# Memory and x queries through one p\*v pass and one output projection per step, with A's weight strips kept in DRAM in SBUF layout

## The chip, the cores and the metric

The kernel runs on one core of a Trainium2 chip. The metric is the device time of one execution in microseconds (us). The core has a matrix engine (TensorE, PE in the profile; its weight loads are PEld), VectorE (DVE), ScalarE (ACT), GpSimd (POOL), and SyncE (SP), which here only issues DMAs. PE multiplies a stationary operand (lhsT), which it has loaded as weights, with a moving one, and writes to PSUM, of which the kernel uses eight banks of 128 x 512 float32. ACT and DVE move results from there to SBUF.

## The reference

Four layers follow each other on x of 2048 rows and 576 columns, each with a layernorm before it and a residual around it: A, B, A, B, with the same weights in both A and both B.

```python
x = x + _A_ref(_layernorm(x), A_wqkv, A_wo)
x = x + _B_ref(_layernorm(x), B_mem0, B_Wq, B_Wk, B_Wv, B_Wo, B_seg_len)
x = x + _A_ref(_layernorm(x), A_wqkv, A_wo)
x = x + _B_ref(_layernorm(x), B_mem0, B_Wq, B_Wk, B_Wv, B_Wo, B_seg_len)
```

A is attention with 32 heads of 18 columns over a dilated window: position s sees s, s-2, ..., s-14. B has 32 heads of 128 columns and goes over 64 segments of 32 rows one after the other. It carries a memory of 8 rows from segment to segment:

```python
mem = mem0
for s in range(n_seg):
    h = concatenate([mem, x[:, s*32:(s+1)*32]])      # 8 + 32 rows
    q, k, v = h @ Wq, h @ Wk, h @ Wv                   # 32 heads x 128
    p = softmax(where(mask, q @ k.T * scale, -1e9))    # memory queries see all; x queries see memory and are causal
    o = (p @ v) @ Wo
    mem = o[:8]                                        # the next segment's memory
    outs.append(o[8:])
```

So a segment of B can't begin its products before the eight output rows of the segment before it are there.

## The kernel before

**Lanes and steps.** Both B layers run at once, as two lanes. Lane 0 is the first B layer and is at segment t in step t; lane 1 is the second and is at segment t - DLY (6 before). There are 64 + 6 = 70 steps, 6 at each end with one lane alone. A tile of 64 rows of layer A (32 tiles for each of the two A layers) is worked in between: the first A layer a few steps ahead of lane 0, the second between lane 0 and lane 1.

**A step of B.** `hT` holds the step's input, transposed, in 80 columns: 32 of lane 0's x, 8 + 8 memory rows of both lanes, 32 of lane 1's x. `qk` (L757, L759) makes q and k: for each head and each of the two, 5 matmuls with 128 x 128 weights and 80 moving columns (40 with one lane), 320 a step in 11 groups of three heads. `vpass` (L803) makes v for blocks of 32 rows, 40 matmuls of 512 columns a block. `scores` runs four times a step: for halves r = 0 and 1 of 16 heads each, and for kinds "m" (memory queries) and "x" (the rows of x). It first puts the mask into the bank by matmuls (L836), then adds q k (L848), column-tiled: four matmuls of 32 output rows side by side. `softmax` goes over three engines: maximum and subtraction on DVE, exponential on ACT, sum and reciprocal on DVE, the scaling on DVE for m and on POOL for x, and a transpose in 32 x 32 blocks on DVE (L712) into `ptm` or `ptx`.

**p\*v and projection.** `pv_m` (L872) runs once per half for the memory queries of both lanes: 48 matmuls of 16 moving columns, row-tiled (32 rows of V each, four side by side, into four banks). `pv_x` (L912) runs once a step for the x queries of both halves: 96 matmuls of 32 or 64 columns. Their results go to the tile `OT`. `oproj` (L946) multiplies OT with wo, 160 matmuls in eight parts. Its columns in step t are the memory queries of step t and the x queries of step t - 1: `pv_x` of a step comes after that step's projection. `mem_out` copies the memory rows into the next step's `hT`, `x_out` adds the x rows to the residual. After the last step one projection for the last x queries follows.

**A's weights.** A's projections don't stay in SBUF. `wload` (L442, L444) brings them in twelve strips per tile (nine of wqkv, three of wo) into a ring of three buffers, with two DMAs a strip: one of rows of up to 508 or 512 bytes for the first 512 rows of the weight, one for the last 64.

**The order.** Nothing is ordered by the engines' own choice: each piece of work is declared as an operation with an engine, an estimated time, dependencies, buffers and a priority (a due time in steps, from the table `PR`). A planner (`_Plan.run`) goes through a modelled time, gives each free engine the ready operation with the lowest priority number whose buffers are free, and writes the instructions in that order. It knows an extra time (`SWITCH`) when PE changes between full-width, column-tiled and row-tiled work.

Of the kernel before, what the change touches and what calls it, by code (L numbers as in the profile page):

```python
# [9 lines left out]
BF16 = mybir.dt.bfloat16  # L10
# [37 lines left out]
class _Op:  # L48
    __slots__ = ("eng", "us", "lat", "fn", "prio", "seq", "acq", "uses", "wait", "next", "mode", "tmin", "done", "lk")


class _Plan:
# [20 lines left out]
    def op(self, eng, us, fn, prio, deps=(), acq=(), uses=(), lat=None, mode="F", tmin=0.0, lk=False):  # L73
# [3 lines left out]
        o.fn, o.prio, o.lat, o.mode, o.tmin, o.lk = fn, prio, lat, mode, tmin, lk  # L77
# [12 lines left out]
    def run(self, log=None):  # L90
# [23 lines left out]
        port = 0.0  # L114
        while left:
# [92 lines left out]
class _K:  # L208
# [37 lines left out]
    def setup(self):  # L246
# [7 lines left out]
        self.x3T = dp.tile([P, NT, 5, T], F32, name="x3T")  # L254

        self.ident = ident = cp.tile([P, P], BF16, name="ident")
        nc.gpsimd.memset(ident[:], 1.0)
        self.sel(ident[:], [[-1, P]], 1, 0, ALU.is_equal, 0.0)
        self.ones = ones = cp.tile([P, P], BF16, name="ones")
# [61 lines left out]
        self.pl.pool("OTm", [None])  # L321
        self.pl.pool("OTx", [None])
        tiles("qk", 7, [P, 3, 2, W80])
        tiles("ptm", 2, [P, 4, 3, 32])
        tiles("ptx", 2, [P, 2, 4, 2, 32])
# [25 lines left out]
        tiles("ot", 1, [P, D])  # L351
        for t_ in tiles("ring", 3, [P, 5, 256]):
            nc.vector.memset(t_[64:128, 4, :], 0.0)
# [3 lines left out]
    def prologue(self):  # L357
# [36 lines left out]
        b = pl.op("PE", 0.3, tr, -2.0, [a], acq=[ps], uses=[x0], mode="R")  # L394
# [8 lines left out]
    def layernorm(self, xT, dep, prio, writer, wus, wacq=(), wuses=(), early=False):  # L403
# [14 lines left out]
        c = pl.op("PE", 0.28, mm, prio, [a, b], acq=[ps], uses=[xs])  # L418
# [16 lines left out]
    def wload(self, src, rows, col0, n, prio, dep):  # L435

        w = self.pl.buf("ring")
        step, last = rows

        def ld(e):  # L440
            d, f = self.nc.sync.dma_start, src[0:1, col0:col0 + 1]
            d(out=w.t[:, 0:4, 0:n], in_=bass.AP(f.tensor, f.offset, [[src.shape[1], P], [step * src.shape[1], 4], [1, n]]))  # L442
            k = min(P, src.shape[0] - last)
            d(out=w.t[0:k, 4, 0:n], in_=src[last:last + k, col0:col0 + n])  # L444
        o = self.pl.op("SP", 0.9, ld, prio, [dep], acq=[w], lat=4.0)
        return w, o

    def a_tile(self, layer, j, dep, due, span):
# [8 lines left out]
        if layer == 1:  # L457
# [9 lines left out]
            b = pl.op("PE", 0.16, tr, pr(0.04), [a], acq=[ps, xT], uses=[x0])  # L467
# [21 lines left out]
        for part in (0, 1, 2):  # L489
            ps = pl.buf("r")  # L490
            o = o_n
            for c in range(5):
                if c % 2 == 0:
                    w, ow = self.wload(self.A_wqkv, (P, 512), part * D + CB[c], 254 if c < 4 else P, pr(Q[1]) - PR["ring"], gate)
                w0 = c % 2 * CB[1]

                def mm(e, c=c, w=w, ps=ps, w0=w0):
                    for kc in range(5):
                        nc.tensor.matmul(ps.t[:, c * T:(c + 1) * T], lhsT=w.t[:, kc, w0:w0 + P], rhs=xn.t[:, kc, :],  # L499
                                         start=(kc == 0), stop=(kc == 4))  # L500
                o = pl.op("PE", 0.15, mm, pr(Q[1] + 0.03 * part), [o, ow], acq=[ps, dst[part]] if c == 0 else (),
                          uses=[xn, w] if c == 0 else [xn, w, ps], lat=0.0 if c < 4 else None)
# [47 lines left out]
        o = o_l = pl.op("PE", 0.4, logits, pr(Q[3]), [o], acq=[psL, e_], uses=[big], mode="C")  # L550
# [26 lines left out]
        for n, (c0, nb) in enumerate(((0, 2), (2, 3))):  # L577
            ps = [pl.buf("r") for _ in range(NQ)]
            b = pl.op("PE", 0.09 * nb, lambda e, ps=ps, c0=c0, nb=nb: spread(ps, c0, nb), pr(Q[4] + 0.02 * n), [b], acq=ps,
                      uses=[e_], mode="R")  # L580
# [20 lines left out]
        for mb in range(5):  # L601
            if mb % 2 == 0:
                w, ow = self.wload(self.A_wo, (CB[1], CB[4]), mb * P, 256 if mb < 4 else 64, pr(Q[6]) - PR["ring"], o_l)
            w0 = mb % 2 * P

            def mm(e, mb=mb, w=w, ps=ps, w0=w0):
                for c in range(5):
                    nc.tensor.matmul(ps.t[:, mb * T:(mb + 1) * T], lhsT=w.t[:, c, w0:w0 + P], rhs=oT.t[:, c, :], start=(c == 0), stop=(c == 4))  # L608
            o = pl.op("PE", 0.15, mm, pr(Q[6]), [o, ow], acq=[ps] if mb == 0 else (),
                      uses=[oT, w] if mb == 0 else [oT, w, ps], lat=0.0 if mb < 4 else None)  # L610
# [8 lines left out]
        def wr2(e, m, rstd):  # L619
# [5 lines left out]
            for o, i, bc in views:  # L625
# [4 lines left out]
                  pr(Q[7]), [o], uses=[xnb])  # L630
        lane = 0 if layer == 1 else 1
# [12 lines left out]
    def finish_out(self, j, prio):  # L644
        nc, pl = self.nc, self.pl
        xb, ot = self.acc[1][j][2], pl.buf("ot")
        a = self.x_done[1][NS * j + NS - 1]
        for n, (c0, c1) in enumerate(((0, 4), (4, 5))):
# [6 lines left out]
            b = pl.op("PE", 0.06 * (c1 - c0), tr, prio, [a], acq=[ps] + ([ot] if n == 0 else []), uses=[xb])  # L655
# [8 lines left out]
        pl.op("SP", 0.5, lambda e: nc.sync.dma_start(out=self.out[0, j * T:(j + 1) * T, :], in_=ot.t[0:T, :]), prio, [o],  # L664
# [13 lines left out]
    def softmax(self, t, ps, e_, n, prio, dep, mul, view, eview, tview, last, pt):  # L678
# [28 lines left out]
        def mult(e):  # L707
# [4 lines left out]
        return pl.op("DVE", 0.14 + 0.00112 * last, lambda e: nc.vector.transpose(out=pt.t[:].rearrange(  # L712
            "p i b q -> p i (b q)" if len(pt.t.shape) == 4 else "p l i b q -> p (l i) (b q)"), in_=tview(e_.t)),
            prio, [o], acq=[pt], uses=[e_])
# [27 lines left out]
    def qk(self, t, g, prio):  # L742
# [8 lines left out]
        def mm(e):  # L751
            pv = ps.t[:, 0:480].rearrange("p (h w k) -> p h w k", h=3, w=2)
            for hh, h in enumerate(heads):
                for wi in range(2):
# [7 lines left out]
                  {h // 8 for h in heads}] if t == 0 else []), acq=[ps, sb], uses=[hT])  # L762
# [209 lines left out]
    def x_out(self, t, dep, prio):  # L972

        nc, pl, psY = self.nc, self.pl, self.psY
        if t < 0:
            return
# [145 lines left out]
```

## Time and profile before

| | |
|---|---|
| median of 3 runs | 2414.54 us (2412.74 to 2416.62) |
| the profiled execution: its own time | 2408.13 us |
| its span, first to last instruction | 2406.4 us |
| mean granted clock of PE | 0.986 |
| matmuls on PE | 70669 |
| PE busy | 2170.3 us (90% of the span) |
| DVE, ACT, POOL busy | 62%, 47%, 42% |
| moved by DMA | 242.42 MB in 508286 packets |

In rows of the profile, "L757" is line 757 of the kernel before, "r<-hT,wq" says that a PSUM bank r is written from tiles hT and wq, "x48" is a count. A row in order of time gives the start, the length up to the last one's end, and in brackets the idle time before it and what ended it. PE's matmuls overlap, so that a group's rate is read from starts. "issue" means that the engine waited for nothing that the profile shows.

### The profile page before, as it was taken

What the parts mean: (1) busy time and instruction counts of PE and PEld (TensorE: products, weight loads), DVE (VectorE), ACT (ScalarE), POOL (GpSimd) and SP (SyncE); (2) the same over time, 40 slices, a digit from 0 to 9 for tenths busy, and PEclk for the clock granted to TensorE, in tenths of its full rate; (3) what the DMA queues carried; (4) which work ended last, traced back from release to release, by engine and by line L of the source; (5) the groups of instructions that cost most, each with busy time, mean ns of one, the idle gap of its engine ahead of it and who ended that gap; (6) DMA issues with size and microseconds to landing.
All of it is one profiled execution on the core that took longest, in us unless ns stands there. A gap on an engine that the chain in (4) does not pass through costs nothing.

```text
span 2406.4 us, 154586 instructions
## 1 busy us (share of the span) xinstructions
PE 2170.3 (90%) x70669; PEld 1862.4 (77%) x70669; DVE 1484.4 (62%) x3777; ACT 1132.6 (47%) x2952; POOL 1006.6 (42%) x1316
## 2 busy tenths in 40 slices
PE   2689999999999999999999999999999999999998
PEld 1577778887788788778787888888888888788876
DVE  3366656666666666666666656666676566665664
ACT  1244444444544444444455444554454445444443
POOL 3142443544454444444454444444444444443320
PEclk9999999999999999999999999999999999999999
DMA  8643443344344434433444344433443443442220
GB/s 244 186 106 84 99 99 96 96 106 108 87 101 103 108 84 110 106 90 94 103 115 101 90 103 107 101 96 101 111 99 92 106 102 93 99 102 62 63 65 11
DMA packets 508286, 242.42 MB, mean 101 GB/s; under 512 B 400744, under 2 KB 503152, under 8 KB 507632
## 3 DMA queue, kind: packets, MB, share of 16 engines
q1 hardware_dynamic: 502800, 213.67, 36.3%
q0 software_dynamic: 4832, 18.88, 2.4%
q8 instruction: 552, 9.04, 1.6%
q14 instruction: 102, 0.84, 0.1%
HBM read 219.59 MB, written 12.85 MB: 97 GB/s over the span
## 4 chain that ended last, share of the span: by engine, by line
PE 85%; issue 6%; DMA 6%; DVE 2%; ACT 1%; SPq 0%; POOL 0%; ACTq 0%; DVEq 0%; POOLq 0%
PE r L757 27%; PE r L946 15%; PE r L803 15%; PE r L759 6%; PE r L499 6%; DMA ring<-in_A_wqkv_dram 6%; PE r L912 3%; PE r L872 2%; PE r L608 2%; PE r L836 2%; PE r L848 2%; PE r L416 2%; PE r L573 1%; PE r L548 1%; PE r L653 0%
## 5 line engine op out<-in xcount | busy, mean ns | idle before, releaser
L757 PE MATMUL r<-hT,wk 128*128 128x80 bf16 (+1 forms) x8960 | 683.9, 200 | 40.0 <-issue 40.0
L757 PE MATMUL r<-hT,wq 128*128 128x80 bf16 (+1 forms) x8960 | 682.3, 200 | 5.5 <-issue 5.5
L757 PEld LDWEIGHTS <-wq 128*128 128x128 bf16 x8960 | 456.2, 100 | 47.2 <-issue 34.6
L757 PEld LDWEIGHTS <-wk 128*128 128x128 bf16 x8960 | 459.8, 100 | 33.8 <-issue 33.8
L946 PE MATMUL r<-OT,wo 128*128 128x80 bf16 (+3 forms) x11360 | 455.2, 198 | 26.6 <-issue 22.1
L243 POOL TENSOR_TENSOR big<-big 128x1280 bf16<-128x1280 bf16 x120 | 242.1, 2017 | 519.0 <-DVE big L243 266.7
L236 ACT ACTIVATE qk<-r 128x480 bf16<-128x480 f32 (+2 forms) x587 | 302.8, 516 | 331.0 <-PE r L759 324.6
L759 PE MATMUL r<-hT,wk_r 128*128 128x80 bf16 (+1 forms) x2240 | 447.3, 200 | 1.9 <-issue 1.8
L759 PE MATMUL r<-hT,wq_r 128*128 128x80 bf16 (+1 forms) x2240 | 447.4, 200 | 0.1
L946 PEld LDWEIGHTS <-wo 128*128 128x128 bf16 x11360 | 414.6, 99 | 39.8 <-issue 34.9
L803 PE MATMUL r<-wv,hT 128*32 128x512 bf16 x5408 | 356.5, 381 | 1.2 <-issue 0.9
L243 POOL TENSOR_TENSOR big<-qT,kT 128x1024 bf16<-128x1024 bf16 x186 | 312.8, 1684 | 50.7 <-ACT kT L236 35.7
L243 POOL TENSOR_TENSOR ex<-ex,sum 128x384 bf16<-128x384 bf16 x140 | 120.1, 858 | 447.8 <-DVE sum L704 377.1
L499 PE MATMUL r<-xn,ring 128*128 128x64 bf16 x4800 | 225.4, 195 | 66.7 <-DMA ring<-in_A_wqkv_dram 62.3
L803 PEld LDWEIGHTS <-hT 128*32 128x32 bf16 x6760 | 168.7, 96 | 131.5 <-issue 4.6
L236 ACT ACTIVATE V<-r 128x512 bf16<-128x512 f32 x303 | 180.7, 596 | 190.2 <-PE r L803 190.0
L236 ACT ACTIVATE OT<-r 128x64 bf16<-128x64 f32 (+2 forms) x615 | 167.7, 336 | 189.2 <-PE r L912 101.1
L499 PEld LDWEIGHTS <-ring 128*128 128x128 bf16 x4800 | 176.0, 99 | 95.5 <-DMA ring<-in_A_wqkv_dram 66.8
L759 PEld LDWEIGHTS <-wk_r 128*128 128x128 bf16 x2240 | 224.8, 100 | 9.9 <-issue 9.6
L759 PEld LDWEIGHTS <-wq_r 128*128 128x128 bf16 x2240 | 224.9, 100 | 0.2 <-issue 0.2
L693 DVE TENSOR_REDUCE nmx<-r 128x4 f32<-128x320 f32 (+1 forms) x280 | 144.4, 516 | 82.4 <-PE r L848 81.5
L238 DVE CAST qk<-r 128x480 bf16<-128x480 f32 (+1 forms) x183 | 117.0, 639 | 109.7 <-PE r L759 105.3
(141 smaller groups left out, 3345.3 us busy)
## 6 DMA issues: line engine op xcount, KB each, us to landing
ring<-in_A_wqkv_dram SPq DMA_DIRECT2D x384, 254.0 KB
ring<-in_A_wo_dram SPq DMA_DIRECT2D x128, 256.0 KB
ring<-in_A_wqkv_dram SPq DMA_DIRECT2D x192, 128.0 KB
ring<-in_A_wo_dram SPq DMA_DIRECT2D x192, 64.0 KB
ring<-in_A_wqkv_dram SPq DMA_DIRECT2D x384, 31.8 KB
x1T<-x SPq DMA_DIRECT2D x32, 160.0 KB
x<-x1T SPq DMA_DIRECT2D x32, 160.0 KB
x3T<-x SPq DMA_DIRECT2D x32, 160.0 KB
```

What stands on the lines that cost most here:

```text
L236: nc.scalar.activation(out=out, in_=in_, func=ACT.Copy, scale=1.0 if scale is None else scale)
L238: (nc.vector if e == "DVE" else nc.gpsimd).tensor_copy(out=out, in_=in_)
L243: (self.nc.vector if e == "DVE" else self.nc.gpsimd).tensor_tensor(out=out, in0=in0, in1=in1, op=op)
L416: nc.tensor.matmul(psf, lhsT=(self.ones if c < 4 else self.ones_h)[:, :], rhs=xs.t[:, c].rearrange("p a t -> p (a t)"), start=(c == 0), st ...
L499: nc.tensor.matmul(ps.t[:, c * T:(c + 1) * T], lhsT=w.t[:, kc, w0:w0 + P], rhs=xn.t[:, kc, :], start=(kc == 0), stop=(kc == 4))
L608: nc.tensor.matmul(ps.t[:, mb * T:(mb + 1) * T], lhsT=w.t[:, c, w0:w0 + P], rhs=oT.t[:, c, :], start=(c == 0), stop=(c == 4))
L693: nc.vector.tensor_reduce(out=m, in_=v, axis=AX.X, op=ALU.max, negate=True)
L757: nc.tensor.matmul(pv[:, hh, wi, a:b], lhsT=wt[:, kc, h * P:(h + 1) * P], rhs=hT.t[:, kc, a:b], start=(kc == 0), stop=False)
L759: nc.tensor.matmul(pv[:, hh, wi, a:b], lhsT=wr[:, (h % 16) * P:(h % 16 + 1) * P], rhs=hT.t[:, 4 + h // 16, a:b], start=False, stop=True)
L803: nc.tensor.matmul(ps.t[c * 32:(c + 1) * 32, :], lhsT=l, rhs=w, start=(kc == 0), stop=(kc == 4))
L912: nc.tensor.matmul(o, lhsT=V[b].t[q4, r, i, :], rhs=p, start=(r == 0 and i == 0 and b == min(V)), stop=(r == 1 and i == 3 and b == 2), ski ...
L946: nc.tensor.matmul(psY.t[:, mb * W80 + c0:mb * W80 + c1], lhsT=self.wo[:, w0:w0 + P], rhs=self.OT[:, h % 16 // 4 * 8 + h // 16 * 4 + h % 4 ...
```

## The change

**One p\*v pass.** `pv_m` and `pv_x` become `pv`, once per half. The transposed probabilities of both kinds lie in one tile `pt` of 80 columns in hT's order (x of lane 0, memory, x of lane 1), and one matmul per head, block of V and row group takes the columns that see the block: 48, 80 or 48. The memory softmax takes the `pt` buffer and the x softmax, whose transpose waits for the memory one's, fills its own columns. `OT` is guarded per half (`OT0`, `OT1`).

**One projection of the same step.** `oproj` takes memory and x queries of step t together; `x_out` follows for step t. The trailing projection goes, `DLY` is 5 instead of 6, and there are 69 steps.

**Masks.** Four column-tiled mask matmuls per score group become one full-width one, with `ident4`, four copies of 32 columns of the identity.

**Strips.** The first tile loads a strip as before (256 columns instead of 254) and stores the buffer to a DRAM tile (`strips`, 12 of 128 x 1280). Later tiles load it from there by one DMA.

**The planner.** PE operations carry their number of matmuls (`mm`), and the modelled time of PE counts instructions: it has pages of 256 instructions, of which the next is fetched in 4.1 us from a point 64 instructions ahead of the page, and PE waits at the page's start if it isn't there. All values of `PR` are new.

**Buffers.** `finish_out` uses the `x0` buffer; `ot`, `ptm` and `ptx` go.

```diff
+    PAGE, AHEAD, FETCH, POS = 256, 64, 4.1, 63
...
+        def fetched(now, us, n2):
+            nonlocal pos, page, avail
+            if not n2:
+                return us
+            t = now
+            while pos + n2 > page:
+                k = page - pos
+                tb = t + us * k / n2
+                tb, us = max(tb, avail), us * (1 - k / n2)
+                hist.append((page, tb))
+                pos, n2 = page, n2 - k
...
+                avail = max(avail, t0 + (t1 - t0) * (page - self.AHEAD - p0) / (p1 - p0)) + self.FETCH
...
+                page += self.PAGE
+                t = tb
+            pos += n2
+            hist.append((pos, t + us))
+            return t + us - now
...
+                        us = fetched(now, us, 2 * o.mm)
...
         def ld(e):
+            if not new:
+                dma(out=w.t[:, 0:5 * n], in_=self.strips[i][:, 0:5 * n])
+                return
+            f, v, k, m = src[0:1, col0:col0 + 1], self.blocks(w, n), min(P, src.shape[0] - last), min(n, src.shape[1] - col0)
+            dma(out=v[:, 0:4, 0:m], in_=bass.AP(f.tensor, f.offset, [[src.shape[1], P], [step * src.shape[1], 4], [1, m]]))
+            dma(out=v[0:k, 4, 0:m], in_=src[last:last + k, col0:col0 + m])
+        o = pl.op("SP", 0.9 if new else 0.5, ld, prio, [dep, self.strip_in.get(i)], acq=[w], lat=4.0)
+        if new:
+            self.strip_new[i] = pl.op("SP", 0.5, lambda e: dma(out=self.strips[i][:, 0:5 * n], in_=w.t[:, 0:5 * n]), prio, [o], uses=[w])
...
-            for c in range(4):
...
-                nc.tensor.matmul(v[c * 32:(c + 1) * 32], lhsT=self.ident[:, 0:32], rhs=msk, start=True, stop=False,
-                                 skip_group_check=True)
+            nc.tensor.matmul(v, lhsT=self.ident4[:], rhs=msk, start=True, stop=False,
+                             skip_group_check=True)
...
-    def pv_m(self, t, r, prio):
...
-    def pv_x(self, t, prio):
...
+    def cols(self, t):
+        on = self.lanes(t)
+        return 0 if on[0] else MC, W80 if on[1] else XC[1]
+
+    def pv(self, t, r, prio):
+        nc, pl = self.nc, self.pl
+        ps, (pt, dep), V = [pl.buf("r") for _ in range(4)], self.PT[r], self.vs(t)
+        on, (c0, c1) = self.lanes(t), self.cols(t)
+        n = c1 - c0
+        blocks = [b for b in V if b == 1 or on[b // 2]]
+        span = {0: (c0, min(c1, XC[1])), 1: (c0, c1), 2: (max(c0, MC), c1)}
+
+        def mm(e):
+            for i in range(4):
+                for b in blocks:
+                    a, z = span[b]
+                    for c in range(4):
+                        q4 = slice(c * 32, (c + 1) * 32)
+                        nc.tensor.matmul(ps[c].t[:, i * n + a - c0:i * n + z - c0], lhsT=V[b].t[q4, r, i, :], rhs=pt.t[q4, i, b, a:z],
+                                         start=(i == 0 and b == blocks[0]), stop=(i == 3 and b == blocks[-1]), skip_group_check=True)
+        o = pl.op("PE", 0.45 if n == W80 else 0.3, mm, prio, [dep] + self.v_done(t, r), acq=ps, uses=[pt, *V.values()], mode="R",
+                  mm=16 * len(blocks))
+        ot = self.ot[r] = pl.buf(f"OT{r}")
+        gate = pl.op("NONE", 0.0, None, prio, [o], acq=[ot])
         for c in range(4):
             s0 = 8 * c + 4 * r
+            def ev(e, c=c, s0=s0):
+                self.copy(e, self.OT[:, s0:s0 + 4, c0:c1], ps[c].t[:, 0:4 * n].rearrange("p (i q) -> p i q", i=4))
+            self.o_ev.append(pl.op(AD_, _evac(4 * n), ev, prio, [gate], uses=[ps[c], ot]))
...
-        m, on = t < self.nsteps, self.lanes(t - 1)
-        c0, c1 = (0 if on[0] else MC if m else XC[1]), (W80 if on[1] else XC[1])
+        c0, c1 = self.cols(t)
...
-        self.x_out(t - 1, dep, t + PR["xo"])
-        self.pv_x(t, t + PR["px"])
+        self.x_out(t, dep, t + PR["xo"])
...
-                s = self.lane_seg(t - 2, lane) if t >= 2 else None
+                s = self.lane_seg(t - 1, lane) if t >= 1 else None
...
-        t = self.nsteps
-        dep = self.oproj(t, [t] * 8)
-        self.x_out(t - 1, dep, t)
...
-DLY = 6
-PR = dict(qk=0.137, qkd=0.03, v1=0.666, v0=1.681, m0=0.241, x0=0.478, m1=-0.393, x1=0.42, pm0=0.738, pm1=0.499,
-          o=0.556, od=0.026, mo=0.239, xo=0.84, px=1.046, v2=1.323, a1=0.673, a1s=3.72, a2=0.689, a2s=2.026,
-          fin=2.616, res=-4.274, ring=-4.575, A=(-0.086, 0.149, 1.189, 0.687, 0.35, 0.699, 0.068, 1.17))
+DLY = 5
+PR = dict(qk=0.239, qkd=0.039, v1=1.392, v0=1.011, m0=0.028, x0=0.262, m1=-0.645, x1=-0.151, p0=1.213, p1=-0.833,
+          o=0.651, od=0.01, mo=0.498, xo=0.715, v2=2.052, a1=1.97, a1s=2.63, a2=0.602, a2s=3.248, fin=2.863,
+          res=-3.898, ring=-6.027, A=(0.14, 0.389, 1.179, 0.534, 0.529, 0.861, 0.134, 1.186))
```

More of the change, by code (lines that the diff above doesn't have):

```diff
@@ L254, in setup @@
         self.x3T = dp.tile([P, NT, 5, T], F32, name="x3T")
+        self.strips = [dp.tile([P, 5 * 256], BF16, name=f"strip{i}") for i in range(12)]
+        self.strip_in, self.strip_new = {}, {}
         self.ident = ident = cp.tile([P, P], BF16, name="ident")
@@ L350, in setup @@
         tiles("fin", 1, [P, 6 * T])
[L351 to L353 removed]
+        for t_ in tiles("ring", 3, [P, 5 * 256]):
+            nc.vector.memset(t_[64:128, :], 0.0)
         pp = self.pool("psum", 1, space=PSUM)
@@ L676, in lanes, with softmax @@
         return [t >= 0 and self.lane_seg(t, l) is not None for l in range(2)]
-    def softmax(self, t, ps, e_, n, prio, dep, mul, view, eview, tview, last, pt):
+    def softmax(self, t, ps, e_, n, prio, dep, mul, view, eview, tview, tout, last, pt, acq, after=None):
         nc, pl = self.nc, self.pl
```

185 lines of the change are left out of this document (69 added, 116 removed).

## The prediction

> **What bounds the kernel now.** I read the page of the profile first: the share of each engine and the chain that ended last.
>
> ```profile
> span 2406.4 us, 154586 instructions
> ...
> PE 2170.3 (90%) x70669; PEld 1862.4 (77%) x70669; DVE 1484.4 (62%) x3777; ACT 1132.6 (47%) x2952; POOL 1006.6 (42%) x1316
> ...
> q8 instruction: 552, 9.04, 1.6%
> ...
> PE 85%; issue 6%; DMA 6%; DVE 2%; ACT 1%; SPq 0%; POOL 0%; ACTq 0%; DVEq 0%; POOLq 0%
> ```
>
> TensorE (PE) is the bound: 85% of the chain, no other engine above 2%. VectorE, the next busiest, has 38% to spare. What is not PE work is "issue" (waiting for nothing that the profile shows) and DMA. The queue q8 carries instructions: 9.04 MB in 552 packets, 16 KB each. PE's 70669 matmuls, each with its weight load, are 141338 instructions, and 141338 / 552 = 256: each packet is one page of 256 PE instructions, 128 matmuls. So next I read the waits of PE alone (total us, times, longest).
>
> ```profile
> PE r L499 <- DMA ring<-in_A_wqkv_dram: 62.3, 38, 10.1
> PE r L912 <- issue: 52.7, 41, 3.1
> PE r L757 <- issue: 45.4, 40, 2.2
> PE r L946 <- issue: 22.1, 37, 1.3
> ...
> PE r L872 <- issue: 5.3, 11, 0.7
> ...
> PE r L499 <- issue: 4.3, 7, 1.3
> ```
>
> The five issue rows sum to 129.8 us in 136 waits. A wait is counted from the modelled end of the last matmul, some 0.18 us after its start, so 136 x 0.18 = 24 us more are lost: about 155 us. That they are page waits shows in the order of time, around the x queries' p\*v (L912) at the end of a step.
>
> ```profile
> 1156.02 0.48 PE L946 MATMUL r<-OT,wo 128*128 128x80 bf16 x9 [1.34 <-issue]
> 1156.34 0.31 PE L499 MATMUL r<-xn,ring 128*128 128x64 bf16 x5
> 1156.48 0.88 PE L946 MATMUL r<-OT,wo 128*128 128x80 bf16 x20
> 1157.30 1.06 PE L912 MATMUL r<-ptx,V 32*128 32x32 bf16 x94
> 1160.05 0.19 PE L912 MATMUL r<-ptx,V 32*128 32x32 bf16 x2 [1.69 <-issue]
> ```
>
> Between the two waits lie 9 + 5 + 20 + 94 = 128 matmuls, exactly one page, in 4.03 us of which 1.69 were waiting. The same 9, 5, 20 and 94 one page apart elsewhere:
>
> ```profile
> 876.89 0.48 PE L946 MATMUL r<-OT,wo 128*128 128x80 bf16 x9 [0.26 <-issue]
> 877.21 0.31 PE L499 MATMUL r<-xn,ring 128*128 128x64 bf16 x5
> 877.36 0.88 PE L946 MATMUL r<-OT,wo 128*128 128x80 bf16 x20
> 878.17 0.91 PE L912 MATMUL r<-ptx,V 32*128 32x32 bf16 x94
> ...
> 881.46 0.19 PE L912 MATMUL r<-ptx,V 32*128 32x32 bf16 x2 [2.38 <-issue]
> ```
>
> 4.57 us. So when matmuls are short, a page takes 4.0 to 4.6 us whatever is in it. Over the steady 53 steps, the windows view counts:
>
> ```profile
> 288.50:2123.50 1835.00, 1713.85 (x55053) 1480.31 (x55044) 1169.38 (x2938) 898.34 (x2306) 827.67 (x1056) 0.99 0.41 100
> ```
>
> 55053 / 128 = 430 pages in 1835 us: 4.27 us a page, inside that span, and 34.6 us and 8.1 pages a step. The delivery of instructions is nearly as hard a bound as PE itself.
>
> **p\*v: 12768 matmuls become 6304.** Before, a two-lane step has 2 x 48 (memory, 16 columns) and 96 (x, 32 or 64 columns). After, it has 2 x 48 of 48 to 80 columns, because the diff puts both kinds of query behind one load of V. 59 two-lane steps x 96 and 10 one-lane steps x 64 give 6304.
>
> ```profile
> 1250.77 0.51 PE L872 MATMUL r<-ptm,V 32*128 32x16 bf16 x48
> 1251.20 0.46 PE L499 MATMUL r<-xn,ring 128*128 128x64 bf16 x10
> ```
>
> ```profile
> L872 PE MATMUL r<-ptm,V 32*128 32x16 bf16 x6432 | 71.5, 168 | 8.0 <-issue 5.3 <-DVE ptm L712 2.1
> L912 PE MATMUL r<-ptx,V 32*128 32x32 bf16 x4480 | 70.3, 177 | 49.5 <-issue 49.4
> L912 PE MATMUL r<-ptx,V 32*128 32x64 bf16 x1856 | 55.1, 189 | 3.4 <-issue 3.4
> ```
>
> 48 take 0.43 us: 9.0 ns each, x 6432 = 58 us. The two groups of 94 above take 0.91 and 1.06 us less the last one's 0.18: 7.8 to 9.4, say 8.6 ns, x 6336 = 54 us. The rate hardly depends on the columns up to 64. Four run side by side on 32 rows each, and a full-width matmul of 80 columns starts every 36 ns (next fence), 9 ns per member of a group of four. So 6304 x 9.0 = 57 us, and 112 - 57 = **55 us saved**. From both sides: 7.8 ns saves 63; the forms of 32 and 64 columns differ by 12 ns, 3 ns for each of a group of four, so 12 ns each saves 36.
>
> **One step fewer (-12).** The lag of the second lane goes from 6 to 5 and the trailing projection goes: 70 steps and a rest become 69, two one-lane steps fuse into one two-lane step.
>
> ```profile
> 1261.15 0.31 PE L757 MATMUL r<-hT,wq 128*128 128x80 bf16 x4
> ...
> 1261.33 0.31 PE L757 MATMUL r<-hT,wk 128*128 128x80 bf16 x4
> ```
>
> ```profile
> 2329.90 0.25 PE L757 MATMUL r<-hT,wq 128*128 128x40 bf16 x4
> ...
> 2330.03 0.25 PE L757 MATMUL r<-hT,wk 128*128 128x40 bf16 x4
> ```
>
> Five matmuls take 0.18 us at 80 columns and 0.13 at 40: 36 and 26 ns. q and k: 640 x 26 go, 320 x 36 come: -5 us. Projection: 480 narrow ones go (27 ns, between the two), 160 wide ones come: -7 us. The lag itself costs nothing: an x segment's output now comes in its own step instead of the next, so layer 3 has as long as before. Bounds -5 and -18.
>
> **Mask matmuls (+13 with the switches).** Four matmuls of 32 columns become one of 128; the stream is the same 320 or 384 columns. What changes is the array's shape around them.
>
> ```profile
> 1237.34 0.20 PE L759 MATMUL r<-hT,wk_r 128*128 128x80 bf16 x1
> 1237.47 0.32 PE L836 MATMUL r<-mask_m,ident 128*32 128x320 bf16 x4
> ```
>
> Going from full width to 32 columns takes 0.13 us where equals follow in 0.036: 0.1 us a switch. A full-width mask between two column-tiled groups adds two switches. The priorities put each x score behind its memory score, so I take two such masks a step: 0.4 us x 69 = +27. Bounds 0 (all behind full-width work) and +55 (all four). One of three row-tiled p\*v groups goes, with two switches: 70 x 0.2 = -14. [...]
>
> **Instruction pages (-120).** 8020 matmuls go (6464 p\*v, 844 mask, 32 score, 320 q/k, 40 V, 320 projection): 62649 stay, 489 pages. A two-lane step loses 108 of 1039 matmuls: 7.3 pages instead of 8.1. Its work was 34.6 us less the waiting 155 / 60 = 2.6: 32 us, 3.9 us a page, under the 4.0 to 4.6. It becomes 32 - 0.8 (p\*v) + 0.2 (switches) = 31.4 us, 4.3 us a page, inside them. A page of q/k alone takes 128 x 36 = 4.6 us and hides the next one. The burst of 96 that L912's 41 waits and L757's 40 stand behind is gone; what stays are bursts of about 50 (p\*v of a half, scores of a half), and a page with one of them takes 0.43 + 80 x 0.036 = 3.3 us, 0.7 to 1.3 short, some of it covered by what PE has queued. All four bursts of a step short by a third of that are 1.6 us a step, 110 us in all; an order that puts V's long matmuls beside the bursts leaves 15. The diff makes the planner count pages, so I take 35 of 155 left. The order itself can't be read off the diff, so both ends stay in the range.
>
> **A's weight strips (-8).** Each strip was two loads of rows of 508, 512 or 256 bytes; after the first tile it is one load from a copy laid out as SBUF has it, 2560 or 1280 bytes a partition. The copy's stores sit on SP behind the landing of their load, hold one of three ring buffers, and the next tile's loads queue behind them.
>
> ```profile
> DMA packets 508286, 242.42 MB, mean 101 GB/s; under 512 B 400744, under 2 KB 503152, under 8 KB 507632
> ```
>
> ```profile
> PE r L499: 48.6, 14
> ...
> L444 SPq DMA_DIRECT2D ring<-in_A_wqkv_dram x16: 465/541/6494, 9.3 to 88.6; - x16
> ```
>
> These last two are of the first 90 us: 48.6 of the 62.3 us of ring waits fall there, while B's weights fill the DMA engines, and the first tile still loads the old way. So the steady gain is at most 62.3 - 48.6 = 14 us; I take 8. At the start twelve stores come on top (3.3 MB) while tiles 2 and 3 load in fewer, longer packets: from -15 to +20, taken as 0, since both act on the same crowded 90 us.
>
> **New waits (+8).** Both softmaxes of a half now stand ahead of its p\*v, and x queries join the loop through the memory.
>
> ```profile
> 1215.35 0.41 PE L848 MATMUL r<-qk 128*32 128x48 bf16 x32
> ...
> 1227.70 0.31 PE L757 MATMUL r<-hT,wq 128*128 128x80 bf16 x4
> ```
>
> ```profile
> 1222.74 0.69 DVE L712 STREAM_TRANSPOSE ptx<-ex 128x512 bf16<-128x512 bf16 x1
> 1225.80 0.23 DVE L966 CAST hT<-r 128x64 bf16<-128x64 f32 x1 [2.36 <-PE r L946]
> ```
>
> From the last x scores (1215.76) to their transposed weights (1223.43) pass 7.7 us. After it, p\*v 0.43, its eviction about as long, the second half of the projection 80 x 0.036 = 2.9, and 1227.70 - 1225.80 = 1.9 for the memory copy and first q (0.7 of it a page wait): 12.7 us in which PE needs other work. It has the projection's first half 2.9, its own 3.3, layer A's 155 matmuls (75 + 25 + 10 + 20 + 20 + 5, a tile a step) at about 0.03, as the ten L499 of row 1251.20 have it (4.7) and the early V pass: near 13. The x pass that used to cover the memory copy is gone, and A and V must. The five one-lane steps at the end have no A left; I estimate a third of its 4.7 us for each, 8 us. Bounds 0 and 1 us a step, 60. Buffers shared now (finish with x0) have a tile's slack.
>
> **The sum**, from the profiled execution's 2408.1 us (span 2406.4): -55 - 12 + 13 - 120 - 8 + 8 = -174, **2234 us**. The median of the runs, 2414.5, is 6 above that execution, within the spread of runs; I say 2235.
>
> **The rivals.**
>
> *The page waits stay.* If the new order leaves the bursts in their own pages, 110 us stay: 2235 + 75 = 2310. For it: after the change the work per page, 4.3 us, is no more than what a page takes to come. Against: its mean rises by 0.4 us.
>
> *Crossing a page costs nothing.* By this the issue waits belong to p\*v itself and only counted work is saved: 2235 + 120 = 2355. Against it: 128 matmuls lie between waits, and most of them stand before L757 and L946 too. [...]
>
> *More than forecast.* Stalls near none, switches hidden, start-up helped: 2235 - 35 - 27 - 15 = about 2155. For it: VectorE, ScalarE and POOL have room.
>
> *Slower: x softmax decides the step.* Place: p\*v of the second half waits for the transposed x weights, and nothing is left for PE. Price: without A's work in the gap 4.7 us a step, x 59 = 277: 2510. It outweighs the gain from 174 / 59 = 2.9 us a step on. Against: 13 us of work for 12.7 us of latency.
>
> **How the numbers follow.** Forecast 0.62, pages stay 0.16, free crossing 0.03, more 0.12, slower 0.07. The runs shown spread by 0.16%, so 0.2% is what can be told from no change; of the slower case 0.01 lies within it. Faster 0.93, same 0.01, slower 0.06. Range 2150 to 2325: from the better case to a little past the page rival.
>
> **What would show it.** 62649 matmuls and about 490 instruction packets; no L912-like group of 96; issue waits of PE summing to 15 to 60 us; ring waits after the first 90 us under 8; p\*v groups of 48 in 0.43 to 0.58 us; a steady step near 31.9 us. A wait of p\*v on VectorE's transposes above 1 us a step, or a page pace still at 4.27 with waits above 100 us, would show me wrong.

## The result, and the profile after

The changed kernel takes 2220.76 us (median of four runs, 2218.52 to 2223.77) against 2413.64 us for the kernel before in the same session (four runs, 2412.62 to 2416.62). The ratio is 0.92, with a 95% interval of 0.9183 to 0.9216: faster by 193 us. The forecast was 2235 us; the profiled execution took 2218.52 us, where the sum had 2234. One execution of the kernel before, in the session whose median is given below as 2403.76 us, took 3987.68 us and is left out of the ratios.

The page of the kernel after, answering to the first fence of the prediction:

```profile
span 2216.7 us, 136592 instructions
...
PE 2092.1 (94%) x62649; PEld 1748.4 (79%) x62649; DVE 1470.5 (66%) x3692; ACT 1153.0 (52%) x2786; POOL 801.3 (36%) x1236
...
DMA packets 147057, 266.04 MB, mean 120 GB/s; under 512 B 18472, under 2 KB 76464, under 8 KB 146480
...
q8 instruction: 489, 8.01, 1.5%
...
PE 87%; DMA 8%; issue 2%; DVE 1%; POOL 1%; ACT 0%; SPq 0%; POOLq 0%; ACTq 0%; DVEq 0%
```

TensorE is still the bound, now 94% busy. The counts came out as worked out from the diff: 62649 matmuls and 489 instruction packets of 16 KB. On the chain, "issue" has gone from 6% to 2%, while DMA has gone from 6% to 8%: six of the eight are loads of strips, most of them stretches of some 5 us all through the execution. The waits of PE in the kernel after (total us, times, longest):

```profile
PE r L543 <- DMA ring<-in_A_wqkv_dram: 27.1, 6, 14.5
PE r L543 <- DMA ring<-strip: 22.8, 28, 8.0
PE r L958 <- issue: 14.2, 22, 1.5
...
PE r L934 <- DVE pt L758: 7.7, 7, 3.4
...
PE r L958 <- ACT OT L266: 5.7, 12, 0.6
PE r L592 <- issue: 5.1, 5, 1.4
```

The same view from 100 us on, where the strips' wait is cut down to its steady part and the smaller page waits come into sight:

```profile
PE r L543 <- DMA ring<-strip: 7.2, 20, 1.0
...
PE r L543 <- issue: 2.5, 6, 1.1
...
PE r L802 <- issue: 1.6, 3, 1.0
PE r L804 <- issue: 1.6, 2, 1.3
```

The five largest issue rows of PE now sum to 14.2 + 5.1 + 2.5 + 1.6 + 1.6 = 25.0 us in 38 waits. Counted as in the prediction, from five rows and with 0.18 us more for each wait, that is 32 us, where before had 155. (With every smaller row, which the lists here leave out, there are 26.1 us in 41 waits after and 136.1 in 148 before.) No row names a p\*v line among them. The steady 53 steps, in the windows view of the kernel after:

```profile
293.10:1982.40 1689.30, 1661.39 (x49315) 1398.06 (x49312) 1166.39 (x2914) 921.93 (x2196) 630.17 (x974) 1.00 0.39 119
```

1689.3 / 53 = 31.9 us a step, where it was 34.6, and 49315 / 128 = 385 pages at 4.39 us each, where it was 4.27. PE is idle for 28 us of that stretch; before it was 121.

### The profile page after: what moved, and what is told of

Same layout as the page of the kernel before. It is cut to its first block, busy times and chain, and to the rows that moved or that the text cites. A ratio compares the mean times of both kernels' runs of the same rounds, so it can differ in the third digit from the quotient of the medians.

```text
span 2216.7 us, 136592 instructions
## 1 busy us (share of the span) xinstructions
PE 2092.1 (94%) x62649; PEld 1748.4 (79%) x62649; DVE 1470.5 (66%) x3692; ACT 1153.0 (52%) x2786; POOL 801.3 (36%) x1236
## 4 chain that ended last, share of the span: by engine, by line
PE 87%; DMA 8%; issue 2%; DVE 1%; POOL 1%; ACT 0%; SPq 0%; POOLq 0%; ACTq 0%; DVEq 0%
PE r L802 28%; PE r L958 16%; PE r L848 14%; PE r L804 7%; PE r L543 7%; DMA ring<-strip 6%; PE r L893 3%; PE r L881 3%; PE r L934 2%; PE r L653 2%; PE r L448 2%; PE r L617 1%; DMA ring<-in_A_wqkv_dram 1%; PE r L592 1%; DMA strip<-ring 1%
## 5 line engine op out<-in xcount | busy, mean ns | idle before, releaser
L802 PE MATMUL r<-hT,wq 128*128 128x80 bf16 (+1 forms) x8832 | 666.7, 199 | 1.4 <-DVE hT L977 0.8
L802 PE MATMUL r<-hT,wk 128*128 128x80 bf16 (+1 forms) x8832 | 665.3, 199 | 1.1 <-issue 1.0
L266 ACT ACTIVATE qk<-r 128x480 bf16<-128x480 f32 (+3 forms) x720 | 382.5, 531 | 284.2 <-PE r L804 244.7
L958 PE MATMUL r<-OT,wo 128*128 128x80 bf16 (+1 forms) x11040 | 420.1, 200 | 21.1 <-issue 14.2
L958 PEld LDWEIGHTS <-wo 128*128 128x128 bf16 x11040 | 398.5, 99 | 31.8 <-issue 29.8
L273 POOL TENSOR_TENSOR big<-qT,kT 128x1024 bf16<-128x1024 bf16 x186 | 319.2, 1724 | 131.5 <-ACT kT L266 130.7
L543 PE MATMUL r<-xn,ring 128*128 128x64 bf16 x4800 | 189.3, 194 | 58.4 <-DMA ring<-in_A_wqkv_dram 27.1
L543 PEld LDWEIGHTS <-ring 128*128 128x128 bf16 x4800 | 159.8, 99 | 83.6 <-DMA ring<-strip 30.3
L266 ACT ACTIVATE OT<-r 128x320 bf16<-128x320 f32 (+1 forms) x350 | 125.9, 421 | 94.5 <-PE r L934 93.8
L268 DVE CAST OT<-r 128x320 bf16<-128x320 f32 (+1 forms) x202 | 87.9, 463 | 105.3 <-PE r L934 103.2
L740 DVE TENSOR_TENSOR r<-r,nmx 128x320 f32<-128x320 f32 (+1 forms) x276 | 147.1, 533 | 9.5
```

The source lines that it names most:

```text
L266: nc.scalar.activation(out=out, in_=in_, func=ACT.Copy, scale=1.0 if scale is None else scale)
L268: (nc.vector if e == "DVE" else nc.gpsimd).tensor_copy(out=out, in_=in_)
L273: (self.nc.vector if e == "DVE" else self.nc.gpsimd).tensor_tensor(out=out, in0=in0, in1=in1, op=op)
L543: nc.tensor.matmul(ps.t[:, c * T:(c + 1) * T], lhsT=self.blocks(w, n)[:, kc, w0:w0 + P], rhs=xn.t[:, kc, :], start=(kc == 0), stop=(kc == 4))
L740: nc.vector.tensor_tensor(out=v, in0=v, in1=m.unsqueeze(len(shp) - 1).to_broadcast(shp), op=ALU.add)
L802: nc.tensor.matmul(pv[:, hh, wi, a:b], lhsT=wt[:, kc, h * P:(h + 1) * P], rhs=hT.t[:, kc, a:b], start=(kc == 0), stop=False)
```

## The experiments

Each is compared with the kernel before on the same chip. That took 2401.38 us beside the moved boundaries and the three runs in which the planner knows of the edit; 2400.75 beside the three edits of p\*v, masks and strips in the same order, where the changed kernel, run again, took 2218.88 (ratio 0.9242, 0.9209 to 0.9274); and 2403.76 beside the planner without the count, the mixed masks and the strips alone, where the changed kernel took 2219.11 (0.9238, 0.9209 to 0.9267). No experiment leaves work of the reference out. Where the planner's costs are changed with an edit, it lays out another order of instructions; so two kinds of runs are told apart, *the planner knows* (another order) and *the same order* (the order of the changed kernel, with other instructions in its places).

> The changed kernel again, as the base on the same chip for the other three, whose instructions stand in exactly its order. Both theories: 0.915 to 0.925 of the kernel before.

> The changed kernel once more, as the base on this chip for the next two. 0.915 to 0.928 of the kernel before.

### p\*v split again, the planner knows

The memory columns and the x columns go as two matmuls behind the same V, so a half's pass has 96 again; all else of the change stays.

```diff
-                    for c in range(4):
+                    for kind in range(2):          # 16 memory columns, then the x columns
+                        for c in range(4):
...
-                   mm=16 * len(blocks))
+                   mm=32 * len(blocks))
```

> The changed kernel with memory and x queries multiplied with V apart again, in the same pass and place: for each head and block 16 memory columns and then the x columns, 96 matmuls a half instead of 48, the planner told. Theory (matmul time and instruction pages both count): 6304 more matmuls x 9 ns = 57 us of PE, 49 more pages (538), issue waits 80 to 160 us: time 2330 to 2390 us. Rival (crossing a page costs nothing, only PE's own time counts): 2265 to 2285 us with issue waits under 45 us.

2405.29 us (ten runs), ratio 1.0019 (0.9996 to 1.0042). The whole gain is gone, and the planner, which knew of each matmul, could not prevent it (the constants of `PR` stayed). The time lies above both ranges; the issue waits, 109 us with every row, are in the theory's. The longest row of its PE waits:

```profile
PE r L945 <- issue: 43.4, 47, 2.3
```

p\*v (L945) again waits for its instructions.

### p\*v split again, the same order

> p*v split again into memory and x columns (96 matmuls a half), the planner not told, order as in the changed kernel. Theory (6304 more matmuls cost 9 ns each on PE, 57 us, and 49 more pages of instructions, waited for in bursts of 96): issue waits 80 to 150 us, 115 to 175 us above f0_after. Rival (pages cost nothing and only PE's time counts, e4_split having lost the rest by its order): 50 to 70 us above it.

2413.15 us (ten runs), ratio 1.0035 (1.0011 to 1.0059): 194 us above the changed kernel on that chip, more than either range. Here nothing but the p\*v matmuls differs, so the 194 us are theirs, and the profile shows where they lie. The waits of PE:

```profile
PE r L969 <- issue: 54.0, 55, 2.5
PE r L945 <- issue: 50.0, 41, 3.2
...
PE r L543 <- issue: 12.6, 17, 1.3
...
PE r L592 <- issue: 7.3, 4, 3.1
```

In these four rows stand 123.9 us in 117 waits, with 0.18 for each 145 us, against 32 in the changed kernel: about 113 us of page waits (125 if every smaller row is counted on both sides). The order of time in the split kernel, then the same place of a step in the changed kernel:

```profile
1308.77 0.91 PE L945 MATMUL r<-pt,V 32*128 32x16 bf16 x96
1309.61 0.46 PE L592 MATMUL r<-big,epad 128*32 128x128 bf16 x19
1312.48 0.29 PE L592 MATMUL r<-big,epad 128*32 128x128 bf16 x1 [2.41 <-issue]
...
1313.20 4.15 PE L969 MATMUL r<-OT,wo 128*128 128x80 bf16 x80
1317.28 1.05 PE L848 MATMUL r<-wv,hT 128*32 128x512 bf16 x16
```

```profile
1210.47 0.54 PE L934 MATMUL r<-pt,V 32*128 32x48 bf16 x48
1210.94 0.46 PE L592 MATMUL r<-big,epad 128*32 128x128 bf16 x20
...
1211.62 3.03 PE L958 MATMUL r<-OT,wo 128*128 128x80 bf16 x80
1214.58 1.22 PE L848 MATMUL r<-wv,hT 128*32 128x512 bf16 x16
```

A group of 96 takes 0.84 us from its start to the next start, the group of 48 only 0.47: 0.37 us on each of 6304 / 48 = 131 groups, 48 us of work. The 96 and the 19 behind them pass in 0.84 + 0.46 = 1.3 us, and the next page is 2.41 us late. And a third part was in no one's sum. The 80 matmuls of L969 take 1317.28 - 1313.20 = 4.08 us, 51 ns each; the same 80 take 1214.58 - 1211.62 = 2.96 us in the changed kernel. The windows view of the split kernel shows why (the third figure from the end is the granted clock):

```profile
1312.90:1315.90 3.00, 3.00 (x50) 3.00 (x48) 2.17 (x8) 0.88 (x3) 0.92 (x2) 0.55 0.03 8
1315.90:1318.00 2.10, 2.10 (x57) 1.71 (x57) 0.56 (x4) 0.26 (x1) 1.35 (x4) 1.00 0.00 0
```

After the late page the clock is 0.55 for some 3 us, and 1.00 behind that. Over the whole execution the mean granted clock of the split kernel, then of the changed one (the kernel before has 0.986):

```profile
core 0: 2413.1 us, clock 0.981
```

```profile
core 0: 2216.7 us, clock 0.997
```

An estimate from these two rows: 0.019 of 2413 us is 46 us of lost clock, 0.003 of 2217 is 7: at most 39 us, less where PE was waiting anyway. 113 + 48 + 39 = 200 against 194 measured: page waits are the largest of the three.

This run makes the burst longer and also adds matmuls in all, so either could be what the waits come from. The trace tells the two apart. Its page waits stand at every 128th matmul, with a drift of 17 over the whole execution: all 120 that are longer than 0.3 us lie within four matmuls of such a boundary. Cut there, the split kernel has 385 pages between 288 and 1980 us. Of the 251 with fewer than 25 p\*v matmuls none is followed by a wait; of the 40 with 25 to 48, 9 are, for 3.4 us; of the 94 with more than 48, 79 are, for 103 us. In the changed kernel, cut in the same way, one page alone has more than 48; of the 67 that hold a whole group of 48, 22 are followed by a wait, 15.5 us in all. So in these two kernels it is what a page holds that makes the next one late, and not how many pages there are.

### The page boundaries moved by half a page, the same order

64 matmuls of 8 columns that nothing reads are put at the start, so that every later boundary falls on another instruction.

```diff
+            for _ in range(64):
+                nc.tensor.matmul(ps.t[:, 64:64 + NM], lhsT=x0.t[0:NM, 0:P], rhs=self.ident[0:NM, 0:NM], start=True, stop=True)
```

> The changed kernel with 64 more matmuls of 8 columns at the very start, in the time in which PE waits for the first strip, and the planner not told of them. Every later instruction stands in the same order, but half a page (128 of 256 instructions) further on, so that page starts fall elsewhere in each step. Theory (PE waits at the start of an instruction page, and the new order has put its short matmuls where the pages let them pass): the issue waits of PE rise from 26 us in 41 waits to 50 to 110 us, and the time from 2221 to 2245 to 2300 us. Rival (the new order spaces the bursts, wherever the pages start, or the waits aren't of pages): issue waits 20 to 45 us, time 2217 to 2228 us.

2224.14 us, ratio 0.9256 (0.923 to 0.9282), an interval that overlaps the two of the changed kernel run again (0.9242 and 0.9238; on the chip of this run it was not run again). This is the rival's case. The largest row of page waits stays near what it was (14.2 us in 22 waits):

```profile
PE r L960 <- issue: 17.3, 24, 1.7
```

A shift of half a page, the only one tried, does not matter in the new order. So the few waits are not owed to boundaries that the planner put in good places.

### The planner without the page count

```diff
-    PAGE, AHEAD, FETCH, POS = 256, 64, 4.1, 63
+    PAGE, AHEAD, FETCH, POS = 1 << 40, 64, 4.1, 63
```

> The changed kernel with an order planned as if instructions came at once (page size without end in the planner), all priorities as in the changed kernel. Theory (the count of pages in the planner keeps the bursts apart): issue waits of PE 50 to 110 us instead of 26 to 33, 20 to 70 us above h0_after. Rival (with 108 matmuls a step fewer the bursts are short enough in any order, as e1_shift suggests): issue waits under 45 us, within 12 us of h0_after.

2220.34 us, ratio 0.9246 (0.9218 to 0.9274): no difference, though the order of PE's 62649 matmuls is another one from the 1512th on. The largest page wait of PE:

```profile
PE r L958 <- issue: 14.2, 27, 1.3
```

It is that of the changed kernel. With p\*v shared and the same tuned constants, an order planned without the count waits as little for them. The constants themselves are all new as well; with those of the kernel before the changed kernel was not run.

### Masks in four tiles again, the same order

```diff
-            nc.tensor.matmul(v, lhsT=self.ident4[:], rhs=msk, start=True, stop=False,
-                             skip_group_check=True)
+            for c in range(4):
+                nc.tensor.matmul(v[c * 32:(c + 1) * 32], lhsT=self.ident[:, 0:32], rhs=msk, start=True, stop=False,
+                                 skip_group_check=True)
```

> The four column-tiled mask matmuls again, but the planner isn't told, so that every other instruction stands where it does in the changed kernel. Theory (a full-width mask behind column-tiled work costs 0.21 us, 176 of 276 stand so; what e2_masks gave away went into its new order): 25 to 37 us below f0_after. Rival (e2_masks had it right and the switch is worth little): 4 to 14 us below it.

2203.74 us (2199.86 to 2208.63), ratio 0.9177 (0.9149 to 0.9204). Each of its four runs is under each of the changed kernel's on that chip (2216.56 to 2224.53). It is 15 us faster than the changed kernel, between what the two sides expected, and beats both kernels. The order of time around one pair of masks, in the changed kernel, then with tiled masks:

```profile
1201.36 0.39 PE L848 MATMUL r<-wv_r,hT 128*32 128x512 bf16 x4
1201.68 0.31 PE L881 MATMUL r<-mask_m,ident 128*128 128x320 bf16 x1
1201.92 0.33 PE L893 MATMUL r<-qk 128*32 128x80 bf16 x16
1202.18 0.90 PE L543 MATMUL r<-xn,ring 128*128 128x64 bf16 x25
...
1203.18 0.38 PE L893 MATMUL r<-qk 128*32 128x48 bf16 x32
```

```profile
1195.05 0.39 PE L848 MATMUL r<-wv_r,hT 128*32 128x512 bf16 x4
...
1195.40 0.28 PE L894 MATMUL r<-qk 128*32 128x80 bf16 x11
...
1196.09 0.90 PE L543 MATMUL r<-xn,ring 128*128 128x64 bf16 x25
...
1197.10 0.41 PE L894 MATMUL r<-qk 128*32 128x48 bf16 x32
```

Behind V's column-tiled matmuls, from the start of V's last four to the scores pass 0.56 us with the full-width mask and 0.35 with the tiled one: 0.21 us for a switch there and back. Behind layer A's full-width matmuls it is 1.00 against 1.01: nothing, as with either mask one step from full width to tiled stands there. Over all masks of both traces the medians say the same: 0.55 against 0.34 us behind V, 0.40 against 0.19 behind other scores, 0.27 against 0.28 behind q and k, which are full width. Going through the trace of the changed kernel, 176 of its 276 masks stand behind column-tiled work; 176 x 0.21 = 37 us. Tiled masks bring 828 matmuls back, 6.5 pages, and the waits of PE in that kernel have grown a little:

```profile
PE r L959 <- issue: 18.2, 30, 1.5
...
PE r L543 <- issue: 6.8, 11, 1.5
```

That is 8.3 us more in these two rows (11 with every row); the remaining 14 of the 37 us were not followed further.

Two variations. With the planner told of tiled masks, so in another order:

> The changed kernel with the mask put in by four column-tiled matmuls again, and the planner told of the three more instructions pairs each. Theory (a full-width mask between column-tiled groups costs two changes of the array's shape): of the 276 masks 176 stand behind column-tiled work; there the stretch from the matmul before to the first score takes 0.40 or 0.55 us where the kernel before took 0.19 or 0.34, so 176 x 0.21 = 37 us come back, and 828 more matmuls cost at most 10: time 2184 to 2196 us. Rival (the change of shape is hidden or the planner's new order gives it away again): 2215 to 2230 us.

2212.47 us, ratio 0.9203 (0.9172 to 0.9234): between the two, and as another order less of a measure of the edit. With the full-width mask kept only where it follows full-width work:

```diff
+            if pl.was == "F":
+                nc.tensor.matmul(v, lhsT=self.ident4[:], rhs=msk, start=True, stop=False, skip_group_check=True)
+            else:
+                for c in range(4):
...
```

> Order of the changed kernel; a mask is put in full width only behind full-width work, else by four column-tiled matmuls. Theory (the array's change of shape is paid only behind column-tiled work, and each of the 300 matmuls saved against f2_masks_order is a bit of a page): 17 to 25 us below h0_after, 2 to 8 below what f2_masks_order had. Rival (pages eat it): 5 to 14 us below h0_after.

2212.36 us (2205.96 to 2220.52), ratio 0.9209 (0.917 to 0.9248), which overlaps the changed kernel's. It has the cheaper form in each place and yet does not beat tiled masks everywhere. Its waits of PE:

```profile
PE r L963 <- issue: 22.7, 31, 2.6
...
PE r L593 <- issue: 9.7, 9, 1.8
```

22.7 + 9.7 us stand where the changed kernel has 14.2 + 5.1, so page waits may have taken part of the gain. But the rows are of the slowest of its four runs (2220.52), and with runs as far apart as these more can't be said.

### The strips loaded the old way

With the planner knowing:

```diff
-        new = i not in self.strip_in
+        new = True
...
-        if new:
-            self.strip_new[i] = pl.op("SP", 0.5, lambda e: dma(out=self.strips[i][:, 0:5 * n], in_=w.t[:, 0:5 * n]), prio, [o], uses=[w])
```

> The changed kernel with each strip of A's weights loaded from its own tensor by two DMAs every time, and nothing stored to DRAM. Theory (steady ring waits fall by some 8 us through the strips, and the twelve stores at the start cost about nothing): 2224 to 2240 us, more ring waits after the first 100 us. First rival (strips are worth nothing, since the loads are hidden anyway): 2217 to 2224 us. Second rival (the stores delay the crowded start by more than the strips save later): 2200 to 2216 us, step 0 beginning earlier than 77 us.

2420.8 us, ratio 1.0079 (1.0048 to 1.0109): above the kernel before, and outside all three ranges. It does not measure the strips, because the order that came of it is a bad one. The longest row of its PE waits:

```profile
PE r L932 <- DVE pt L756: 94.4, 44, 3.6
```

p\*v waits 94.4 us for the transposed weights, seven times in the changed kernel and 44 times here. This is the mechanism of the rival on the slower side, at a part of its price. In the same order, with loads alone undone:

> A's strips loaded the old way by two DMAs each, no copies, but the planner counts as if they were copies, so that the order is that of the changed kernel. Theory (on the chip the longer packets are worth little, and e3_nostrip lost its time to another order, in which p*v waits for the x softmax): 5 to 30 us above f0_after, ring waits up by as much, waits of p*v on VectorE under 15 us. Rival (e3_nostrip shows what the strips are worth): 120 us or more above f0_after.

2288.98 us, ratio 0.9534 (0.9507 to 0.9561): 70 us slower than the changed kernel. The waits of PE:

```profile
PE r L540 <- DMA ring<-in_A_wqkv_dram: 104.8, 85, 11.7
PE r L650 <- DMA ring<-in_A_wo_dram: 11.5, 16, 1.3
```

116 us for strips, against 27.1 + 22.8 for those of L543 in the changed kernel: 66 us more, while the issue rows fall from 26 us to 6, which fits pages that come while PE waits for a strip. Neither side expected 70. So the new order relies on the strips' loads: from 120 us on PE waits 7.2 us for them in the changed kernel, in 20 waits, and here 54.1 us in 72 for the old loads of wqkv alone. Whether the longer rows do it or the one DMA in place of two was not tried apart. Last, the strips' copies alone, put into the kernel before in its own order (the store is issued on SP within the load's operation, behind its landing):

> The kernel before with A's strips alone (stored from the first tile, loaded by one DMA afterwards), its planner and order unchanged. Theory (its order leaves the loads time, and only the 12.6 us of ring waits after the first 100 us can go): 4 to 20 us below the kernel before. Rival (strips are worth what f3_nostrip_order showed, in any order): 50 to 80 us below it.

2428.51 us, ratio 1.0101 (1.0049 to 1.0153): 25 us slower than the kernel before, where both sides expected it faster. The longest of its PE waits, and then B's first q matmuls in the order of time, there and in the kernel before:

```profile
PE r L927 <- issue: 55.4, 38, 2.4
PE r L772 <- issue: 46.4, 39, 2.6
PE r L961 <- issue: 29.7, 47, 1.8
```

```profile
90.72 0.29 PE L772 MATMUL r<-hT,wq 128*128 128x40 bf16 x4
```

```profile
74.05 0.32 PE L757 MATMUL r<-hT,wq 128*128 128x40 bf16 x4
```

B begins 16.7 us later. The stores now stand on SP ahead of the next loads, and the waits of SP in the first 95 us show what that does: at the store (L450) it stands until the strip has landed, 36.9 us for the strips of wqkv, in the row below, and 18.7 for those of wo.

```profile
SPq L450 <- DMA ring<-in_A_wqkv_dram: 36.9, 9, 9.9
```

In the changed kernel the store is an operation of its own and B begins at 76.95 us, so most of the 16.7 us are the price of this form of the edit. Later the three issue rows, in the same three places of the order as L912, L757 and L946 before, have 131.5 us where those had 120.2. From 100 us on PE waits 2.8 us for strips, where the kernel before waited 12.6 for its ring, and all its issue rows have 155 us, where those of the kernel before had 136. So the strips did save waits, and in this order, with its 155 us of issue waits, nothing of them came back.

## Why the prediction was right, point by point

- **Instruction pages (-120): the size was right, the reason in part wrong.** 155 us became 32, so -123. "The diff makes the planner count pages" was my ground for taking 35 of 155, and it fell: without the count the time is the same, and with the boundaries elsewhere too. What did it is the other half of that part, the burst of 96 that is gone: put back in the same order, it returns about 113 us of page waits. The bound of 110 us left came from supposing that all four bursts of about 50 in a step make a page late by a third of 0.7 to 1.3 us; of the pages that hold a whole p\*v group of 48 one in three does, by 0.7 us, and the others hardly ever. That what PE has queued covers some of the 0.7 to 1.3 us was supposed, and no run shows it.
- **p\*v (-55): the mechanism right, the size a little high.** A group of 48 takes 0.47 us with 48 to 80 columns, 9.8 ns a matmul, where the row of 16 columns gave 9.0: 131 x 0.47 = 62 us, so the saving is 112 - 62 = 50, within 36 to 63.
- **Masks and switches (+13): too low for the masks.** I took two masks a step with 0.2 us for each, 27 us. The 0.2 us a mask is what the rows show (0.21), but 176 are behind column-tiled work, not 138: 37 us. Undoing the edit returns 15 net. The edit cost time, as the prediction had it. The -14 for a p\*v group fewer has not been measured by itself.
- **Strips (-8).** From 100 us on, the ring waits were 12.6 us and are 7.2 (row above), so -5; all of them went from 62.3 to 49.9. From 90 us on, as the prediction counted, 10.6 us are left, more than the 8 that it named as a sign. The rows before and after hide what the runs showed: undone in the new order they cost 70 us, added to the old one they brought no gain.

The kernel before from 100 us on, for the 12.6:

```profile
PE r L499 <- DMA ring<-in_A_wqkv_dram: 12.6, 23, 1.2
```

- **One step fewer (-12)** was not tried by itself, since it does not come apart from the sharing.
- **New waits (+8).** p\*v waits 7.7 us for the transposed weights where L872 had 2.1 in the kernel before, and the projection 5.7 for the evicted output where L946 had 3.2: 8 us more. That the size is right is luck. It was reckoned for the five one-lane steps at the end, where layer A has no work left; of the 7.7 us 5.4 stand in the first 222 us, in the one-lane steps at the start, and about 2 at the end.
- **The sum.** The terms as measured are -50, -12 (untested), +23 (37 - 14, the 14 untested), -123, -5 and +8, together -159; with the start's ring waits (-7) -166. The execution went from 2408.1 to 2218.5, -190. The 24 us between are about the size of the lost clock, estimated as above: 0.014 of 2406.4 us is 34, 0.003 of 2216.7 is 7, so 27 at most, less what fell into waits. That it closes the sum so well is arithmetic, not a run. The prediction had no term for the clock; the masks (10 too low), p\*v (5) and the strips (3) went the other way. That it still came within 16 us is in part luck.
- **The rivals.** *The page waits stay* (2310) fell: 32 us are left. *Crossing a page costs nothing* (2355) fell: by it, the split in the same order would have cost the 48 us of its work, and it cost 194. It did cost nothing behind the 224 pages without p\*v of the split kernel, which take 4.6 us on average and none of which is followed by a wait; where 115 matmuls passed in 1.3 us, the wait behind them was 2.41 us. *More than forecast* (2155): the time went 14 us towards it. The better kernel, with tiled masks at 2203.74, is on that side too. *Slower* fell for this order, but one of the orders tried shows its wait, 94.4 us of it.

What decided is the sharing of p\*v: undone alone, in the same order, it takes back the whole gain. The reverse, the sharing alone put into the kernel before, was not run. The shares of the parts do not add: strips and sharing each return 70 and 194 us when undone, and together more than the 182 us (2400.75 - 2218.88) that there are on that chip.

## What to carry to other kernels

Where short matmuls come in bursts, count the instructions before the array's cycles, and join two that read the same weights: here 45 of the 67 pages that hold a whole group of 48 had no wait behind them, against 15 of the 94 with more than 48 in the split kernel, and that was worth more than twice the array's own saving (113 us against 48). Before an edit saves matmuls by another array shape, look at what stands ahead of each; behind tiled work the one full-width matmul here cost 0.21 us more than the four tiled ones. Undo each part in the order of the whole as well as alone, for a part can be worth 70 us in one order and nothing in another.

## What the hardware showed that was not expected

In the split kernel a wait of PE of more than 2 us mostly cost twice. After the one of 2.41 us the granted clock was 0.55 over the next 3 us, and 80 projection matmuls took 4.08 us, where the changed kernel, in the same place and at a granted clock of 1.00, takes 2.96: 1.1 us lost to the clock beside the 2.41. It is no single case: from 100 us on the clock of the split kernel falls to 0.50 in 25 stretches, nearly all of 3.4 us. Such a stretch begins during the wait or within 1.5 us after it for 12 of its 15 waits above 2 us, for 12 of the 44 between 1 and 2 us, and for none of the 100 below 1 us. The worst clock of all was in the order that waited most for VectorE (the strips the old way, the planner knowing), 0.965 over 2418.2 us. That speaks for PE's standing still, and not the page, as what the clock answers to; it was not tried apart.

In the old order the number of packets meant little. The strips' copies alone took them from 508286 to 147122 there, with 267.08 MB to move where it had been 242.42, and this made the kernel no faster: 2428.51 against 2403.76 us.
